# Block attention before two gated layers on one core: the head pairs of the attention taken two at a time, with the planner pricing each change of TensorE tiling

## The chip, the cores and the metric

One core of a Trainium2 chip runs the whole kernel. The metric is the device time of one execution in microseconds (us); the time before is the median of three runs, 610.3 us (610.02 to 610.71).

## What is computed

The reference, cut to what matters (B 2, H 8, S 768, D 64, block 32, window 16):

```
k_sum = k.reshape(B, H, nb, block, D).max(axis=3)
v_sum = v.reshape(B, H, nb, block, D).mean(axis=3)
scores_l = where(|i - j| < window, scale * q @ k.T, -1e9)
scores_s = scale * q @ k_sum.T + log(block)
a = softmax(concat(scores_l, scores_s))
x = a @ concat(v, v_sum)              # 1536 tokens x 512
h = x @ w_in;  g = h * clip(h + 3, 0, 6) / 6;  x = g @ w_out
h = x @ w_in2; g = h * cos(h);                 out = g @ w_out2
```

All is float32. The two layers have 512 inputs, 2048 inner units and 512 outputs.

## The kernel before, in words

**Attention.** Heads are taken in pairs: a pair's two heads lie on partitions 0 to 63 and 64 to 127, and there are four pairs (p) for each of two batches (b). The 768 tokens are cut into three parts (h) of 256, so there are 24 units (b, h, p). Only keys near the diagonal count, so each 64 query rows meet 120 columns: 96 keys (CW) of their window and 24 block maxima. A unit (`att`, L505) runs: `score` on TensorE (L511 to L518, eight small products of 64 rows by 64 columns, two instructions each, so 16 records) into the two PSUM tiles s; four times a masked minimum on VectorE (L529) and an exponential on ScalarE that also adds up its row (L537); a small addition on GpSimd (L546), the reciprocal (L551) and the scaling (L555, GpSimd or VectorE); four transposes (`trans`, L562) into t, a copy to pt (L567, ScalarE or VectorE); `pv` (L569 to L574, 16 records, 120 rows by 64 columns) into o; and the split of the result into a rounded high part xh (L580) and a remainder xl (L582).

**Loads and sums.** K, V and Q come by DMA from SP's queue (`load_k`, `load_v`, `load_q`, L453 to L468). At the first part of a batch, `k_prep` (L494) takes the block maxima of K on VectorE (L497) and `vsum_pe` (L470) the block means of V on TensorE: 24 small records (L477), a copy, a second product of two records (L482), another copy; `fill` (L489) then spreads the means into vw on GpSimd or ScalarE.

**Layers.** The 1536 tokens form three blocks of 512 (four tiles of 128). In each of two layers and for each of four groups of four chunks of 128 inner units, every block runs `g1` (L657: 12 products for each chunk, three for each quarter of the 512 inputs, so the first quarter needs head pair 0 only), `post` (L676, the gate on ScalarE, VectorE and GpSimd), and `g2` (L726, four output tiles of 12 products). The first block is cut in two halves of 256 tokens. The weights are loaded and converted chunk by chunk in two halves each (`weights`, L609; L618, L622, L627 and the splits). A block needs the attention of its own tokens only: block 0 needs parts 0 and 1 of batch 0, block 1 part 2 of batch 0 and part 0 of batch 1.

**Order.** `Plan` (L121) works out, before the kernel is built, when each operation starts on which engine, from the costs and priorities written at each `op` call and in the table T (L77): at each moment an engine takes the ready operation with the lowest priority whose buffers are free. Each engine, and SP's queue of DMAs, then runs its list in that order. The units stand in the order of the priorities: in batch 0 those of part 1 run interleaved with those of part 0, one pair behind; the rest follow part by part. Where the plan leaves TensorE idle before T's `busy` (42 us), `run` (L337) puts small products on the identity there (`idle`, L434), whose results nobody reads. Buffers are rings: z (Q) 3, e (the scores) 3, sm 4, pt 2, vs 2, r 2, and single PSUM tiles for t and o.

Of the kernel before, what the change touches and what calls it, by code (L numbers as in the profile page):

```python
# [14 lines left out]
ACTF = mybir.ActivationFunctionType  # L15
ALU = mybir.AluOpType
AX = mybir.AxisListType

P = 128
# [43 lines left out]
def consts():  # L63
# [53 lines left out]
class Op:  # L117
    __slots__ = ("engs", "fn", "prio", "port", "seq", "wait", "after", "ready", "takes", "uses", "start", "eng", "took")


class Plan:  # L121
# [10 lines left out]
    def op(self, engs, fn, prio, r=(), w=(), take=(), port=0.0):  # L132
        o = Op()
        o.engs, o.fn, o.prio, o.port, o.seq = engs, fn, prio, port, len(self.ops)
# [87 lines left out]

    def refine(self):
# [19 lines left out]
    def order(self):  # L243
# [6 lines left out]
        free["DMA"] = T["d0"]  # L250

# [11 lines left out]
        while events:  # L263
# [11 lines left out]
            for e in names:  # L275
# [79 lines left out]
def body(ctx: ExitStack, tc: tile.TileContext, q, k, v, w_in1, w_out1, w_in2, w_out2, ident_d, mask_d, avg_d, out):  # L355
# [34 lines left out]
    c_r = slots("r", 2, [P, TOK], later=T["n2"])  # L390
# [62 lines left out]
    def load_q(b, h, p, prio):  # L453
        z = Buf(c_z)
        dma(lambda: z.t, lambda: q[b, p][:, HT * P * h:HT * P * h + HT * P], 0.54, prio, w=[z], take=[z])
        return z
# [13 lines left out]
    def vsum_pe(vw, prio):  # L470

        bank, x, y = Buf(c_h), Buf(c_vs), Buf(c_y)

        def mm(e):
            for s in range(NS):
                a, g = 2 * (NS - 1 - s), s % 4 * QD
                nc.tensor.matmul(out=bank.t[g:g + QD, 0:P], lhsT=avg[0:CW, a:a + QD], rhs=vw.t[0:CW, s, :],  # L477
                                 start=(s < 4), stop=(s >= NS - 4), tile_position=(0, g))

        op({"PE": 0.85}, mm, prio, r=["avg", (vw, 0)], w=[bank], take=[bank, x, y])  # L480
        op({"ACT": 0.2, "DVE": 0.2}, lambda e: copy(e, y.t, bank.t[:, 0:P]), prio, r=[bank], w=[y])
        op({"PE": 0.25}, lambda e: nc.tensor.matmul(out=bank.t[CW:P, P:2 * P], lhsT=avg[:, AW:AW + QD], rhs=y.t,  # L482
                                                    start=True, stop=True, tile_position=(0, CW)),
           prio, r=["avg", y], w=[bank])
        op({"ACT": 0.2, "DVE": 0.2}, lambda e: copy(e, x.t[CW:CE, :], bank.t[CW:CE, P:2 * P]), prio, r=[bank],
           w=[(x, 0), (x, 1)])
        return x

    def fill(x, vw, prio):  # L489
        op({"POOL": 1.5, "ACT": 1.55},  # L490
           lambda e: copy(e, vw.t[CW:CE, :, :], x.t[CW:CE, :].rearrange("p (u f) -> p u f", u=1).to_broadcast([NB, NS, P])),
           prio, r=[(x, 0), (x, 1)], w=[(vw, CW)], take=[vw])
# [12 lines left out]
    def att(b, h, p, kw, z, vw, prio, banks):  # L505
        sp = [Buf(banks) for _ in range(2)]
        e_, sm, pt, tp, res = Buf(c_e), Buf(c_sm), Buf(c_pt), Buf(c_t), Buf(c_o)
        N4 = 2 * HT
        subs = [(i, u, o) for i in range(HT) for u in range(2) for o in range(2)]

        def score(e):  # L511
            for i, u, o in subs:
                f = slice(D * o, D * o + D)
                a = i * P + u * SUB
                nc.tensor.matmul(  # L515
                    out=sp[o].t[u * SUB:u * SUB + SUB, i * CE:i * CE + CE], lhsT=z.t[f, a:a + SUB],
                    rhs=kw.t[f, 2 * (HT * h + i) + u, :], start=True, stop=True,
                )  # L518

        op({"PE": 0.58}, score, prio,  # L520
           r=[z, (kw, "own"), (kw, "sum")], w=sp, take=[*sp, e_, sm])
        for i in range(HT):
            t = HT * h + i
            mk = mask[:, 0 if t == 0 else (2 if t == TB - 1 else 1), :]
            for o in range(2):
                x = 2 * i + o
                op(
                    {"DVE": 0.2},
                    lambda e, i=i, o=o, x=x, mk=mk: nc.vector.tensor_tensor_reduce(  # L529
                        out=e_.t[:, x, :], in0=sp[o].t[:, i * CE:i * CE + CE], in1=mk,  # L530
                        scale=-0.125, scalar=3.0e38, op0=ALU.add, op1=ALU.min, accum_out=sm.t[:, x:x + 1],
                    ),
                    prio, r=[sp[o], "masks"], w=[(e_, x), (sm, x)],
                )
                op(
                    {"ACT": 0.38},
                    lambda e, x=x: nc.scalar.activation(  # L537
# [286 lines left out]
```

## Time and profile before

| what | value |
|---|---|
| median of the runs | 610.3 us (610.02 to 610.71) |
| the profiled execution | 610.45 us |
| its span, first to last instruction | 608.7 us |
| TensorE (PE) busy | 602.1 us, 99% |
| VectorE (DVE) busy | 387.2 us, 64% |
| ScalarE (ACT) busy | 268.8 us, 44% |
| GpSimd (POOL) busy | 347.0 us, 57% |
| records of products on the identity | 146, the last at 45.10 us |
| granted TensorE clock | 1.00 throughout |

The busy times are sums over a span with two very different stages: attention mixed with the first blocks of the first layer (up to 118 us), and the layers alone. Matmul records overlap their successors, so what one costs TensorE is read from its start to the start of the next.

### The profile page before, as it was taken

Reading aid. Unit: us, or ns where it says so; the run is one execution under the profiler, and the core shown is the slowest. Engines: PE = TensorE matmul, PEld = TensorE weight load, DVE = VectorE, ACT = ScalarE, POOL = GpSimd, SP = SyncE. Lnnn points to the kernel's source line nnn. Section 1 sums busy time; section 2 is a strip of 40 time slices with the busy share of each in tenths; the row PEclk is TensorE's granted clock in tenths of the full one; section 3 lists DMA queues with packets and bytes.
Section 4 is the critical chain, followed back from the end, with each engine's and each line's share of the span. In section 5 each row is a group of like instructions: output and inputs, shape, how many; then the busy total and the mean of one; then the engine's idle time right before and its main releaser. Section 6 shows DMA issues by size and latency. Waiting matters only on the chain.

```text
span 608.7 us, 9662 instructions
## 1 busy us (share of the span) xinstructions
PE 602.1 (99%) x3636; PEld 498.6 (82%) x3636; DVE 387.2 (64%) x724; ACT 268.8 (44%) x585; POOL 347.0 (57%) x366
## 2 busy tenths in 40 slices
PE   9999999999999999999999999999999999999997
PEld 8878877788888888888888888888888888888886
DVE  3599894443852258523993589857984897574562
ACT  2698886533421114301351547654752363343240
POOL 2588784555853438623688398656864577443340
PEclk9999999999999999999999999999999999999999
DMA  9978950042420004300440013301320020000112
GB/s 224 269 240 246 255 184 22 1 138 70 138 70 0 1 7 167 105 0 1 140 137 0 1 69 104 104 2 68 105 103 2 1 103 1 1 2 0 70 42 97
DMA packets 28334, 50.07 MB, mean 82 GB/s; under 512 B 14464, under 2 KB 17920, under 8 KB 28288
## 3 DMA queue, kind: packets, MB, share of 16 engines
q1 hardware_dynamic: 28144, 49.40, 26.4%
q8 instruction: 28, 0.46, 0.3%
q14 instruction: 18, 0.15, 0.1%
q10 hardware_dynamic: 144, 0.07, 0.0%
HBM read 46.31 MB, written 3.15 MB: 81 GB/s over the span
## 4 chain that ended last, share of the span: by engine, by line
PE 94%; DVE 2%; POOL 1%; ACT 1%; issue 1%; DVEq 0%; POOLq 0%; ACTq 0%
PE acc L743 25%; PE s L743 18%; PE h L667 8%; PE h L668 8%; PE h L669 8%; PE o L669 3%; PE t L669 3%; PE o L667 3%; PE t L667 3%; PE o L668 3%; PE t L668 3%; PE acc L434 2%; PE s L515 2%; PE o L573 2%; PE t L564 2%; PE h L477 1%
## 5 line engine op out<-in xcount | busy, mean ns | idle before, releaser
L405 POOL TENSOR_SCALAR g<-r 128x512 fp32r<-128x512 f32 (+1 forms) x81 | 61.9, 764 | 135.4 <-DVE r L718 40.8
L410 POOL TENSOR_TENSOR g<-r,g 128x512 fp32r<-128x512 f32 (+1 forms) x73 | 100.5, 1377 | 7.3 <-ACT g L403 2.8
L699 ACT ACTIVATE n<-h,bias 128x512 f32<-128x512 f32 (+1 forms) x60 | 39.3, 656 | 141.3 <-PE h L669 139.3
L743 PE MATMUL acc<-g,w 128*128 128x512 f32 (+1 forms) x432 | 96.0, 370 | 0.0
L667 PE MATMUL h<-xh,w 128*128 128x512 f32 (+1 forms) x240 | 92.5, 386 | 0.0
L668 PE MATMUL h<-xl,w 128*128 128x512 f32 (+1 forms) x240 | 90.0, 375 | 0.0
L669 PE MATMUL h<-xh,w 128*128 128x512 f32 (+1 forms) x240 | 90.0, 375 | 0.0
L743 PEld LDWEIGHTS acc<-g,w 128*128 128x128 f32 x432 | 75.3, 188 | 14.3 <-issue 0.8
L703 DVE SCALAR_TENSOR_TENSOR r<-n,h 128x512 f32<-128x512 f32 (+1 forms) x60 | 38.7, 646 | 56.8 <-ACT n L699 31.0
L743 PE MATMUL acc<-w,g 128*128 128x512 f32 x288 | 69.2, 389 | 0.0
L743 PE MATMUL s<-w,g 128*128 128x512 f32 x288 | 69.2, 389 | 0.0
L410 POOL TENSOR_TENSOR w<-cf,w 128x512 fp32r<-128x512 f32 x44 | 64.1, 1460 | 3.3 <-ACT w L403 1.6
L743 PEld LDWEIGHTS acc<-w,g 128*128 128x128 f32 x288 | 54.1, 188 | 11.2
L743 PEld LDWEIGHTS s<-w,g 128*128 128x128 f32 x288 | 54.0, 188 | 11.2
L627 DVE SCALAR_TENSOR_TENSOR cf<-cu,cf 128x512 uint32<-128x512 uint32 x64 | 60.0, 955 | 0.4
L618 ACT ACTIVATE cu<-raw 128x512 f32<-128x512 f32 x64 | 42.9, 670 | 38.5 <-DVE cf L627 23.7
L622 DVE TENSOR_SCALAR cf<-raw 128x512 uint32<-128x512 uint32 x64 | 47.3, 755 | 11.8 <-POOL w L410 11.6
L667 PEld LDWEIGHTS h<-xh,w 128*128 128x128 f32 x240 | 45.1, 188 | 9.9 <-issue 1.7
L711 POOL TENSOR_SCALAR n<-n 128x512 f32<-128x512 f32 x45 | 31.8, 707 | 37.3 <-ACT n L699 37.2
L669 PEld LDWEIGHTS h<-xh,w 128*128 128x128 f32 x240 | 45.1, 188 | 8.2
L668 PEld LDWEIGHTS h<-xl,w 128*128 128x128 f32 x240 | 45.1, 188 | 7.8
L405 POOL TENSOR_SCALAR w<-cf 128x512 fp32r<-128x512 f32 x41 | 31.4, 770 | 30.3 <-DVE cf L627 23.2
(95 smaller groups left out, 1054.7 us busy)
## 6 DMA issues: line engine op xcount, KB each, us to landing
raw<-in_w_in_dram SPq DMA_DIRECT2D x32, 512.0 KB, 4.1
raw<-in_w_out_dram SPq DMA_DIRECT2D x32, 512.0 KB, 3.7
kw<-in_k_dram SPq DMA_DIRECT2D x8, 576.0 KB, 6.0
vw<-in_v_dram SPq DMA_DIRECT2D x8, 576.0 KB, 9.3
z<-in_q_dram SPq DMA_DIRECT2D x24, 128.0 KB, 5.7
out_dram<-part SPq DMA_DIRECT2D x8, 256.0 KB, 2.0
out_dram<-kw SPq DMA_DIRECT2D x3, 256.0 KB, 2.0
out_dram<-kw SPq DMA_DIRECT2D x2, 128.0 KB, 1.7
```

The costliest lines, as they stand in the source:

```text
L405: eng[e].tensor_scalar(out=out, in0=in_, scalar1=scale, scalar2=0.0, op0=ALU.mult, op1=ALU.add)
L410: eng[e].tensor_tensor(out=out, in0=in0, in1=in1.bitcast(F32), op=ALU.subtract)
L618: lambda e, raw=raw, u=u: nc.scalar.activation(out=u.t, in_=raw.t.bitcast(F32)[:, :, 1], func=ACTF.Prelu, scale=2.0 ** -112, alpha=2.0 ** 32),
L622: lambda e, raw=raw, f=f: eng[e].tensor_scalar(out=f.t.bitcast(U32), in0=raw.t[:, :, 0], scalar1=2.0 ** -29, scalar2=7.0, op0=ALU.mult, op ...
L627: lambda e, u=u, f=f: nc.vector.scalar_tensor_tensor(out=f.t.bitcast(U32), in0=u.t.bitcast(U32), scalar=3, in1=f.t.bitcast(U32), op0=ALU.l ...
L667: nc.tensor.matmul(out=o, lhsT=wh, rhs=hi, start=(kk == 0), stop=False)
L668: nc.tensor.matmul(out=o, lhsT=wh, rhs=lo, start=False, stop=False)
L669: nc.tensor.matmul(out=o, lhsT=wl, rhs=hi, start=False, stop=(kk == KT - 1))
L699: op({"ACT": t(fixed, 0.43)}, lambda e: nc.scalar.activation(out=out(), in_=in_(), func=func, **kw), pr, r=rd, w=wr, take=take)
L703: op({"DVE": t(0.09, 0.56)}, lambda e: nc.vector.scalar_tensor_tensor(out=out(), in0=a(), scalar=s, in1=b(), op0=o0, op1=o1), pr, r=rd, w= ...
L711: op({"POOL": t(0.16, 0.47), "DVE": t(0.07, 0.265)}, lambda e: eng[e].tensor_scalar(out=n(), in0=n(), scalar1=1.0, scalar2=-MAGIC, op0=ALU ...
L743: nc.tensor.matmul(out=o, lhsT=l, rhs=r, start=(c == 0 and z == 0), stop=(c == GS - 1 and z == 2))
```

## The change

Attention takes pairs of head pairs: `att` now gets one or two of them (ny). The 24 units become 13: part 0 of batch 0 as pair 0, pair 1, then pairs 2 and 3 together; from there on two pairs each. One `score` call issues 32 records for two pairs, and one `pv` call 32 records; transposes and their copies stay one call for each pair. Every exponential of the second pair is taken without its row sum, and one VectorE reduction over 4 x 120 elements takes the place of its four row sums. `vsum_pe` works on two V tiles: 48 records in its first call, and one second product of twice the columns. Q for two pairs comes by one DMA, and the copies to xh and xl are of twice the width. At part 0 of a batch, K and V are loaded two by two. The ring sizes and T change with it. The plan gets a price for each change of tiling on TensorE.

```diff
-    A0=6.982, AS=1.584, mask=-12.92, kp=-20.41, qp=-33.47, lk=-17.33, lq=-11.81, lv=-4.43, vs=33.64, vss=-16.92,
-    vsp=-29.27, wl=-1.64, wc=-25.07, g0=20.77, gi=7.33, pp=27.42, fill=-9.73, DVE=1.348, POOL=0.497, cold=5, d0=0.9,
-    warm=9, tail=1, lagq=1, nraw=3, ncf=2, n=5, w2=2, n2=3, g2=3, nz=3, busy=42, slack=0.2, vpe=-7.47, avg=-27.4,
+    A0=5.118, AS=1.568, mask=-8.22, kp=-14.19, qp=-15.92, lk=-15.36, lq=-11.42, lv=-4.09, vs=37.77, vss=27.87,
+    vsp=-18.03, wl=-15.78, wc=-15.19, g0=20.42, gi=5.51, pp=17.22, fill=-28.29, DVE=1.348, POOL=0.572, cold=5, d0=0.9,
+    warm=9, tail=1, lagq=3, nraw=3, ncf=2, n=5, w2=2, n2=3, g2=3, nz=2, nr=1, busy=42, slack=0.2, vpe=-45.26,
+    avg=-8.5,
...
+    def change(a, b):
+        if a == b:
+            return 0.0
+        return (0.165 if a > 1 else 0.0) + (0.19 if b > 1 else 0.1 if b else 0.0)
...
+                if e == "PE":
+                    cost += self.change(mode, o.mode)
+                    mode = o.mode
...
-    c_z = slots("z", T["nz"], [P, HT * P], pool=ap)
+    c_z = slots("z", T["nz"], [P, 2, HT * P], pool=ap)
-    c_vs = slots("vs", 2, [P, P], pool=ap)
-    c_y = slots("y", 1, [P, P], pool=ap)
+    c_vs = slots("vs", 1, [P, 2, P], pool=ap)
+    c_y = slots("y", 1, [P, 2, P], pool=ap)
-    c_e = slots("e", 3, [P, 2 * HT, CE], pool=ap)
-    c_sm = slots("sm", 4, [P, 4 * HT])
+    c_e = slots("e", 2, [P, 4 * HT, CE], pool=ap)
+    c_sm = slots("sm", 2, [P, 8 * HT])
-    c_r = slots("r", 2, [P, TOK], later=T["n2"])
+    c_r = slots("r", T["nr"], [P, TOK], later=T["n2"])
...
-        op({"PE": 0.85}, mm, prio, r=["avg", (vw, 0)], w=[bank], take=[bank, x, y])
+        op({"PE": 1.36}, mm, prio, r=["avg", *((vw, 0) for vw in vws)], w=[bank], take=[bank, x, y], mode=4)
...
-        op({"PE": 0.58}, score, prio,
-           r=[z, (kw, "own"), (kw, "sum")], w=sp, take=[*sp, e_, sm])
+        op({"PE": 0.41 * ny}, score, prio,
+           r=[z, *((kw, x) for kw in kws for x in ("own", "sum"))], w=sp, take=[*sp, e_, sm], mode=2)
...
+            add = x < N4
             op(
-                    {"ACT": 0.38},
+                {"ACT": 0.38 if add else 0.2},
...
+                    **(dict(accum_out=sm.t[:, N8 + x:N8 + x + 1]) if add else {}),
...
+            if y:
+                op({"DVE": 0.55},
+                   lambda e, y=y, a=a: nc.vector.tensor_reduce(
+                       out=sm.t[:, a], in_=e_.t[:, y * N4:y * N4 + N4, :], axis=AX.X, op=ALU.add),
+                   prio, r=[(e_, x) for x in xs], w=sums, port=0.3)
...
-        op({"PE": 0.62}, pv, prio, r=[pt, (vw, 0), (vw, CW)], w=[res], take=[res])
+        op({"PE": 0.44 * ny}, pv, prio, r=[*pts, *((vw, x) for vw in vws for x in (0, CW))], w=[res], take=[res], mode=3)
...
-    for p in range(NP + T["lagq"]):
-        units += [(0, 0, p)] * (p < NP) + [(0, 1, p - T["lagq"])] * (p >= T["lagq"])
-    units += [(b, h, p) for b in range(B) for h in range(NH) for p in range(NP) if b or h > 1]
+    units = [(0, 0, 0, 1), (0, 0, 1, 1), (0, 0, 2, 2)]
+    units += [(b, h, p, 2) for b in range(B) for h in range(NH) for p in range(0, NP, 2) if b or h]
...
+        both = (p, p + 1) if h == 0 and p % 2 == 0 else ()
+        for y in both:
+            kws[y], ks = load_k(b, y, pr + (y - p) * AS * HT * (ny < 2) + T["lk"])
+            k_prep(kws[y], ks, pr + T["kp"])
+        z = load_q(b, h, p, ny, pr + T["lq"])
+        for y in both:
+            vws[y] = load_v(b, y, pr + T["lv"])
+        if both:
+            x = vsum_pe([vws[y] for y in both], pr + T["vpe"])
+            for y in both:
+                fill(x, y - p, vws[y], pr + T["fill"])
```

## Rows read from the trace of the kernel before

**Rows 1.** Busy time by stretch: stretch, length, each engine's busy us (instructions), clock, DMA share, GB/s.

```profile
30.00:46.00 16.00, 14.64 (x219) 12.26 (x217) 15.65 (x47) 14.89 (x46) 13.31 (x15) 1.00 0.79 241
46.00:94.00 48.00, 47.40 (x668) 39.73 (x669) 44.21 (x163) 42.13 (x152) 36.62 (x44) 1.00 0.78 219
94.00:118.00 24.00, 24.00 (x246) 17.81 (x244) 9.50 (x47) 14.20 (x48) 12.38 (x16) 1.00 0.03 8
118.00:604.00 486.00, 486.00 (x2146) 402.42 (x2145) 304.25 (x402) 184.04 (x291) 273.92 (x269) 1.00 0.17 57
```

**Rows 2.** Waits of PE from 46 us to the end: us, times, longest.

```profile
PE s L515 <- DVE sm L529: 0.3, 1, 0.3
PE t L564 <- POOL e L555: 0.2, 1, 0.2
```

**Rows 3.** Timeline of PE, 0 to 42 us: start, first start to last end, instruction.

```profile
19.03 4.90 PE L434 MATMUL acc<-ident 128*128 128x64 f32 x42
23.86 0.86 PE L477 MATMUL h<-vw,avg 96*32 96x128 f32 x24
...
29.84 1.45 PE L434 MATMUL acc<-ident 128*128 128x64 f32 x12
...
35.14 0.39 PE L667 MATMUL h<-xh,w 128*128 128x256 f32 x1
```

**Rows 4.** Timeline of PE around one score group and one pv group, 59 to 61.5 us.

```profile
59.22 0.64 PE L515 MATMUL s<-kw,z 64*64 64x120 f32 x16
59.79 0.38 PE L667 MATMUL h<-xh,w 128*128 128x256 f32 x1
60.01 0.28 PE L668 MATMUL h<-xl,w 128*128 128x256 f32 x1
60.13 0.28 PE L669 MATMUL h<-xh,w 128*128 128x256 f32 x1
...
60.49 0.28 PE L669 MATMUL h<-xh,w 128*128 128x256 f32 x1
60.70 0.69 PE L573 MATMUL o<-pt,vw 120*64 120x64 f32 x16
61.31 0.39 PE L667 MATMUL h<-xh,w 128*128 128x256 f32 x1
```

**Rows 5.** Timeline of PE in windows that cut a group short, and one whole.

```profile
63.30 0.54 PE L515 MATMUL s<-kw,z 64*64 64x120 f32 x12
...
63.30 0.64 PE L515 MATMUL s<-kw,z 64*64 64x120 f32 x16
...
60.70 0.51 PE L573 MATMUL o<-pt,vw 120*64 120x64 f32 x10
...
79.54 0.64 PE L477 MATMUL h<-vw,avg 96*32 96x128 f32 x16
```

**Rows 6.** Groups of PE's instructions from 46 to 118 us: count, busy us, mean ns.

```profile
L573 PE MATMUL o<-pt,vw 120*64 120x64 f32 x272 | 11.7, 228 | 0.0
...
L515 PE MATMUL s<-kw,z 64*64 64x120 f32 x238 | 9.8, 275 | 0.5 <-DVE sm L529 0.3
...
L477 PE MATMUL h<-vw,avg 96*32 96x128 f32 x96 | 3.4, 277 | 0.0
L482 PE MATMUL h<-y,avg 128*32 128x128 f32 x8 | 1.6, 285 | 0.0
```

**Rows 7.** VectorE: a group of 30 to 94 us, one of 94 to 125, two reductions in the timeline.

```profile
L627 DVE SCALAR_TENSOR_TENSOR cf<-cu,cf 128x512 uint32<-128x512 uint32 x14 | 15.2, 1088 | 0.0
...
L529 DVE CUSTOM_DVE_ANT_0 e<-s,mask 128x120 f32<-128x120 f32 x16 | 3.6, 279 | 1.9 <-PE s L515 1.9
...
59.51 1.00 DVE L497 TENSOR_REDUCE ks<-kw 128x12 f32<-128x384 f32 x2
```

**Rows 8.** ScalarE: the reads of the row sums, a group of 30 to 94 us.

```profile
L537 ACT ACTIVATION_READ_ACCUMULATOR e<-e,sm 128x1 f32 x59 | 11.1, 188 | 0.0
```

**Rows 9.** SP's queue, timeline: start, us from first to last issue's end.

```profile
27.29 0.44 SPq L437 DMA_DIRECT2D vw<-in_v_dram  x1
```

More of the change, by code (lines that the diff above doesn't have):

```diff
@@ L117 @@
 class Op:
-    __slots__ = ("engs", "fn", "prio", "port", "seq", "wait", "after", "ready", "takes", "uses", "start", "eng", "took")
+    __slots__ = ("engs", "fn", "prio", "port", "seq", "wait", "after", "ready", "takes", "uses", "start", "eng", "took", "mode")
 class Plan:
@@ L562, in trans @@
-        def trans(e):
-            for x in range(N4):
-                nc.tensor.transpose(out=tp.t[0:CE, x * P:(x + 1) * P], in_=e_.t[:, x, :], identity=ident)
-        op({"PE": 0.44}, trans, prio, r=[(e_, x) for x in range(N4)], w=[tp], take=[tp, pt])
-        op({"ACT": 0.49, "DVE": 0.6}, lambda e: copy(e, pt.t[0:CE, :], tp.t[0:CE, :]), prio, r=[tp], w=[pt])
-        def pv(e):
-            for i, u, o in subs:
-                f = slice(D * o, D * o + D)
-                a, c = (2 * i + o) * P + u * SUB, i * P + u * SUB
-                nc.tensor.matmul(out=res.t[f, c:c + SUB], lhsT=vw.t[0:CE, 2 * (HT * h + i) + u, f],
-                                 rhs=pt.t[0:CE, a:a + SUB], start=True, stop=True)
@@ L576, in att @@
-        op({"PE": 0.62}, pv, prio, r=[pt, (vw, 0), (vw, CW)], w=[res], take=[res])
+            for y in range(ny):
+                for i, u, o in subs:
+                    f = slice(D * o, D * o + D)
+                    a, c = i * P + u * SUB, (y * HT + i) * CE
+                    nc.tensor.matmul(
+                        out=sp[o].t[u * SUB:u * SUB + SUB, c:c + CE], lhsT=z.t[f, y, a:a + SUB],
+                        rhs=kws[y].t[f, 2 * (HT * h + i) + u, :], start=True, stop=True,
+                    )
@@ new lines, in att, with trans @@
+        for y in range(ny):
+            xs = range(y * N4, y * N4 + N4)
+            sums = [(sm, N8 + x) for x in xs]
+            a = slice(N8 + y * N4, N8 + y * N4 + N4)
+            if y:
[3 more added lines that the diff above has]
+                   prio, r=[(e_, x) for x in xs], w=sums, port=0.3)
+            op(
+                {"POOL": 0.2},
+                lambda e, a=a: nc.gpsimd.tensor_scalar(
+                    out=sm.t[:, a], in0=sm.t[:, a], scalar1=1.0, scalar2=1e-9, op0=ALU.mult, op1=ALU.add
+                ),
+                prio, w=sums,
+            )
+            op({"DVE": 0.09}, lambda e, a=a: nc.vector.reciprocal(out=sm.t[:, a], in_=sm.t[:, a]), prio, w=sums)
+            op(
+                {"POOL": 1.05, "DVE": 0.57},
+                lambda e, y=y, a=a: eng[e].tensor_tensor(
+                    out=e_.t[:, y * N4:y * N4 + N4, :], in0=e_.t[:, y * N4:y * N4 + N4, :],
+                    in1=sm.t[:, a].rearrange("p (x u) -> p x u", u=1).to_broadcast([P, N4, CE]), op=ALU.mult,
+                ),
+                prio, r=sums, w=[(e_, x) for x in xs], port=0.5,
+            )
+            def trans(e, y=y, xs=xs):
+                for x in xs:
+                    c = (x - y * N4) * P
+                    nc.tensor.transpose(out=tps[y].t[0:CE, c:c + P], in_=e_.t[:, x, :], identity=ident)
+            op({"PE": 0.425}, trans, prio, r=[(e_, x) for x in xs], w=[tps[y]], take=[tps[y], pts[y]], mode=1)
+            op({"ACT": 0.49, "DVE": 0.6}, lambda e, y=y: copy(e, pts[y].t[0:CE, :], tps[y].t[0:CE, :]), prio, r=[tps[y]],
+               w=[pts[y]])
@@ new lines, in pv @@
+        def pv(e):
+            for y in range(ny):
+                for i, u, o in subs:
+                    f = slice(D * o, D * o + D)
+                    a, c = (2 * i + o) * P + u * SUB, (y * HT + i) * P + u * SUB
+                    nc.tensor.matmul(out=res.t[f, c:c + SUB], lhsT=vws[y].t[0:CE, 2 * (HT * h + i) + u, f],
+                                     rhs=pts[y].t[0:CE, a:a + SUB], start=True, stop=True)
+        op({"PE": 0.44 * ny}, pv, prio, r=[*pts, *((vw, x) for vw in vws for x in (0, CW))], w=[res], take=[res], mode=3)
@@ L577, in att @@
         j, i = divmod(b * TB + HT * h, QT)
         c = slice(i * P, (i + HT) * P)
[L579 to L583 removed]
+        hi, lo = xh[j][:, p:p + ny, c], xl[j][:, p:p + ny, c]
@@ L585, in body, with both @@
+        his, los = ([(x, j, p + y, t) for y in range(ny) for t in range(i, i + HT)] for x in ("xh", "xl"))
+        def both():
+            return res.t[:, 0:ny * HT * P].rearrange("p (y c) -> p y c", y=ny)
+        op({"ACT": 0.07 + 0.21 * ny, "DVE": 0.07 + 0.27 * ny}, lambda e: copy(e, hi, both()), prio, r=[res], w=his)
+        op({"DVE": 0.06 + 0.27 * ny}, lambda e: sub(e, lo, both(), hi), prio, r=[res, *his], w=los)
     A0, AS = T["A0"], T["AS"]
```

131 lines of the change are left out of this document (52 added, 79 removed).

## The prediction

> **What bounds the kernel.** I read first the busy time by stretch [rows 1]: from 118 to 604 us TensorE is busy without a gap, and from 94 to 118 as well; from 46 to 94 it lacks 0.6 us in 48. The granted clock is 1.00, the 2.4 GHz level, in every stretch, so no time is to be had from the clock. Next the waits of TensorE from 46 us on [rows 2]: two, 0.5 us together. So from 46 us to the end TensorE works through a fixed list in a fixed order, and whatever is taken out of that list ends the kernel earlier by as much, as long as the other engines still deliver in time. Before 46 us it is otherwise. The timeline [rows 3] shows products on the identity, which nobody reads: 42 of them between 19.03 and the V sums at 23.86, 12 more from 29.84 and 14 later ones. There TensorE is waiting for loads and for other engines, and taking products out gives only more of these. The layers begin at 35.14.
>
> The second thing to see in [rows 1] is VectorE: 15.65 of 16 us up to 46, 44.21 of 48 up to 94, then only 9.50 of 24. It is nearly full exactly where the change gives it more to do.
>
> **What a group of small products costs TensorE.** In the stretch of [rows 4], products of the layers on 256 columns start 0.12 us apart (60.01 to 60.13). A score group takes 0.57 us from its start to the next instruction (59.22 to 59.79). The product before a small group takes 0.21 until the group starts (60.49 to 60.70), 0.09 too much, and the first after it 0.22 (59.79 to 60.01), 0.10 too much. A pv group takes 0.61 (60.70 to 61.31). Inside a group the pace is quicker than these figures: cutting the score group after 12 of 16 records shortens it by 0.10, so 0.025 a record and 0.40 for 16; cutting a pv group after 10 shortens it by 0.18, so 0.03 a record and 0.48 for 16 [rows 5]. What is left is the price of entering and leaving: 0.57 + 0.19 - 0.40 = 0.36 us for scores, 0.61 + 0.19 - 0.48 = 0.32 for pv. For the V sums, 24 records take 0.86 and 16 take 0.64 [rows 3, 5], so 0.0275 a record and 0.66 for 24. Their ends overlap the successor by 0.07, as the score group's do (0.64 against 0.57), so the group takes 0.79, and its price is 0.79 + 0.19 - 0.66 = 0.32.
>
> **The change on TensorE.** After 46 us stand 238 score records (14 whole groups and the rest of one), 272 of pv (17 groups), 96 of V sums (4 groups) and 8 of their second product (4 groups) [rows 6]. Two pairs in one call leave the records and take away every second group: 7 x 0.36 = 2.5, 8.5 x 0.32 = 2.7, 2 x 0.32 = 0.6. Of the second products two go, at least the 0.19 at their edges, 0.4; their columns remain. Sum 6.2 us. Some groups already stand directly behind another small group and have no edge to the layers, so I take 5.5; the ends are 6.2 and, if the next paragraphs go wrong, nothing. The transposes stay as they are, one call a pair, and cost what they did. The groups before 46 us save as much each, but there it turns into waiting.
>
> **The ramp.** The new priorities put part 0 of batch 0 first: before, part 1 came in between, and the last V of the batch was issued only at 27.29 [rows 9], behind the first weights (its priority 18.4 against 13.7 for the first chunk; after the change 7.3 against 7.1 for the first chunk and 8.5 for the second, worked out from the two tables T). So pairs 2 and 3 should have their V some us earlier and the first half of block 0 can start earlier. What this can give at most is the slack after 29.84: 26 products on the identity at 0.12 (1.45 for 12 [rows 3]) is 3.1 us, and the idle time of 30 to 46 is 1.36 [rows 1], together 4.5; the 4.83 us from 19.03 to 23.86 could come on top, since both V tiles are now fetched before the first sum. Against it stands that a pair of pairs waits for the later of two loads, that its z is freed only after both scores, with the loads behind it in SP's queue, and that only two e tiles of double size are left. I take -3.0, two thirds of the 4.5; the ends are -9.3 and a loss of two further waits of 4.83, that is +9.7.
>
> **VectorE.** It gets 11 reductions over 480 elements. The nearest row is a reduction over 384, 1.00 us for two [rows 7]; so between 0.50 and 0.63 each, and I take 0.56, 6.2 us in all. Behind 94 us only 16 of the 96 masked minima are left, four units [rows 7], so 20 of the 24 units come before; in the new form these hold nine reductions, 9 x 0.56 = 5.0 us, against 0.35 + 3.79 = 4.1 us idle between 30 and 94 [rows 1]. And that stretch is to become some us shorter. What can give way: the weights of the second group, converted early. The 14 conversions of 30 to 94 us [rows 7] are six more than the first group's four chunks need, 1.09 us each, 6.5 us that can move past 94, where VectorE is half idle. I count +1.5 us of TensorE waiting for VectorE, between 0 and 4.
>
> **ScalarE** loses 44 reads of row sums, at most 0.19 us each [rows 8]; it has 42.13 of 48 us in the middle stretch [rows 1] and doesn't set the pace, so I count nothing; if VectorE were short, the copies that may go to either would move over. The wider copies to xh and xl and the 11 Q loads fewer move the same bytes: nothing, hidden behind TensorE's list. One r tile in place of two before 118 us: r is held for one chunk's gate, and block 0's chunks pass between attention groups, further apart than a gate lasts, so nothing; without that cover g1 would wait for its PSUM bank.
>
> **Sum** for the profiled execution: 610.45 - 5.5 - 3.0 + 1.5 = 603.45. That execution lies 0.15 above the median of the runs, so 603.3 us.
>
> **Rivals.**
> *VectorE becomes the bound up to 94 us.* For it: the fill of [rows 1] and the reductions. Against it: the conversions that can move. Then TensorE gains only behind 94, where four score groups become two and at least as many pv groups, 2 x 0.36 + 2 x 0.32 = 1.4, the ramp gains nothing, and the stretch grows by 5.0 - 4.1 = 0.9: 610.45 + 0.9 - 1.4 = 609.95. The Trainium skill, page "VectorE: DVE Perf Modes", section "Rules for kernel authors", speaks for this one: it calls the tensor_reduce the slowest operation of that engine and advises against it on a hot path. By that rule the sum would be this 609.95 and not 603.3; the trace agrees that it is slow, half a microsecond for 384 elements [rows 7], but the path is hot only as far as the conversions can't move.
>
> *The ramp gets longer, and the kernel slower.* Pairs taken together wait for the later of their two V loads and fills. Place: the first pv of pairs 2 and 3 of part 0, then the first of part 1, which needs the pt tiles of that one. Price: a wait like that of 19.03 to 23.86 twice, 9.7 us. Then 610.45 + 9.7 - 5.5 = 614.6. It decides from the point at which the ramp loses more than the 5.5; one such wait would still leave about no change. Against it: the priorities of K and V.
>
> *The ramp gives all of its slack* and VectorE doesn't hold anything up: 610.45 - 5.5 - 4.5 and half of the 4.83 is 598.0.
>
> *The change doesn't save the edges*, because what costs is each group's first and last records wherever they stand. Then only the ramp and VectorE remain, 610.45 - 3.0 + 1.5 = 609.0. The even pace inside a group [rows 5], across changes of row and column halves, speaks against it.
>
> **Chances.** The forecast, 600 to 607: 0.62. The full ramp: 0.13. VectorE as the bound: 0.12, half of it just past the border of a measurable gain. The long ramp: 0.10. No edges saved: 0.03. A measurement of this kernel can tell 0.2%, 1.2 us, from no change. Faster by more than that: 0.62 + 0.13 + 0.06 + 0.02 = 0.83; within: 0.07; slower: 0.10. The range leaves out the long ramp, half of the VectorE case and the far end of the full ramp: 596.5 to 609.1.
>
> **What would show it.** In the trace after: 13 score groups, 11 of them of 32 records and 1.04 us long, pv groups of 32 in 1.17 us, with the same 0.09 and 0.10 at their edges; 11 new reductions of 0.50 to 0.63 us on VectorE and 52 reads of row sums on ScalarE; the first product of a layer before 35 us and fewer than 146 products on the identity; the waits of TensorE after 46 us below 2 us. The forecast is wrong if TensorE waits for VectorE by more than 4 us between 30 and 94, if the layers begin later than 35 us, or if a group of 32 takes twice a group of 16.

## The result, and the profile after

The changed kernel takes 618.58 us (median of four runs), the kernel before 610.5 in the same comparison: 1.0126 times as long, with a 95% interval of 1.0111 to 1.0142. It is slower by about 8 us where the forecast was 7 faster. One of the four runs, 637.6 us, is of a slower kind that the kernel before shows too (628 us in other comparisons); the medians in this document count such runs (without it this one is 617.67), the ratios leave them out. The profiled execution took 619.48 us with a span of 617.7 and a mean clock of 0.994; the remaining two took 617.65 and 617.67 at a mean clock of 1.00, so the loss is there without a lower clock.

Busy time by stretch of the kernel after (stretch, length, busy us and instructions of PE, PEld, DVE, ACT, POOL, then the granted clock, the DMA share and GB/s), beside [rows 1]:

```profile
0.00:30.00 30.00, 28.83 (x340) 27.01 (x340) 11.84 (x54) 11.37 (x35) 7.54 (x19) 1.00 0.91 236
30.00:46.00 16.00, 15.62 (x265) 13.79 (x264) 14.85 (x51) 14.71 (x42) 12.53 (x14) 1.00 0.74 236
46.00:94.00 48.00, 42.83 (x584) 37.38 (x581) 41.62 (x127) 34.41 (x91) 32.58 (x42) 0.93 0.76 218
70.00:80.00 10.00, 8.79 (x127) 7.05 (x128) 7.79 (x40) 6.94 (x24) 3.84 (x6) 0.66 0.71 204
94.00:118.00 24.00, 24.00 (x269) 20.03 (x268) 11.78 (x64) 14.88 (x49) 12.07 (x18) 1.00 0.09 24
118.00:131.00 13.00, 13.00 (x120) 10.62 (x119) 5.81 (x25) 7.50 (x21) 5.97 (x9) 1.00 0.00 1
131.00:612.00 481.00, 481.00 (x2150) 398.27 (x2150) 306.60 (x404) 182.88 (x289) 277.05 (x267) 1.00 0.17 57
```

From 46 to 94 us TensorE now lacks 5.2 us of 48 (0.6 before), and its mean clock there is 0.93 of full speed. The window cut closer, from 70 to 80 us, has a clock of 0.66. From 94 us on TensorE is full again, as before. The waits of TensorE from 46 us on, against [rows 2], no longer make half a microsecond but 4.8:

```profile
PE t L595 <- POOL e L585: 1.6, 1, 1.6
PE s L538 <- issue: 1.5, 1, 1.5
PE t L595 <- DVE e L585: 1.0, 1, 1.0
PE s L538 <- DVE sm L551: 0.5, 1, 0.5
PE h L708 <- DVE r L744: 0.2, 1, 0.2
```

The ramp, from the timeline of PE (start, first start to last end, instruction), against [rows 3]:

```profile
8.87 8.47 PE L447 MATMUL acc<-ident 128*128 128x64 f32 x74
17.18 0.60 PE L595 MATMUL t<-ident,e 128*120 128x128 f32 x4
17.71 0.64 PE L538 MATMUL s<-kw,z 64*64 64x120 f32 x16
...
21.19 3.56 PE L447 MATMUL acc<-ident 128*128 128x64 f32 x30
24.68 1.52 PE L492 MATMUL h<-vw,avg 96*32 96x128 f32 x48
...
30.40 0.69 PE L606 MATMUL o<-pt,vw 120*64 120x64 f32 x16
...
37.20 1.05 PE L538 MATMUL s<-kw,z 64*64 64x120 f32 x32
38.19 2.45 PE L447 MATMUL acc<-ident 128*128 128x64 f32 x20
40.56 1.15 PE L606 MATMUL o<-pt,vw 120*64 120x64 f32 x32
```

The first thing to see is 74 records on the identity in a row, 8.47 us. The transposes at 17.18 that stand behind them have had their input since 12.67, by the timeline of DVE:

```profile
11.77 0.90 DVE L585 TENSOR_TENSOR e<-e,sm 128x480 f32<-128x480 f32 x1
```

So TensorE makes products that nobody reads for 4.5 us while work is ready. The groups of the kernel after show the same in sum, 236 such records against 146, and the new reductions:

```profile
L447 PE MATMUL acc<-ident 128*128 128x64 f32 x236 | 27.9, 275 | 0.0
...
L560 ACT ACTIVATION_READ_ACCUMULATOR e<-e,sm 128x1 f32 x52 | 9.8, 188 | 0.0
...
L572 DVE TENSOR_REDUCE sm<-e 128x4 f32<-128x480 f32 x11 | 7.1, 644 | 3.1 <-ACT e L560 3.1
```

**An account of TensorE.** I went through the timeline of PE from start to start up to the last pv group and put each stretch to one of three: attention's products (with the 18 at the very start), products of the layers, and slack, which is waits and products on the identity. Slack is split at the first product of a layer. "Rest" is the span less attention's products and slack.

The last pv group itself counts to the rest. All runs but the first two are described in the next section.

| profiled execution | span | attention's products | slack before the first layer product | slack after it | rest |
|---|---|---|---|---|---|
| before | 608.7 | 52.7 | 16.8 | 2.1 | 537.1 |
| after | 617.7 | 48.9 | 21.3 | 11.2 | 536.3 |
| before, divisor 0.23 (e2) | 607.1 | 54.0 | 14.4 | 1.3 | 537.4 |
| after, divisor 0.23 (e1) | 610.6 | 48.7 | 15.0 | 9.7 | 537.2 |
| e1 with the old table (e6) | 609.0 | 48.6 | 15.4 | 7.9 | 537.1 |
| e1 with four single units first (e9) | 606.6 | 48.6 | 12.0 | 9.5 | 536.5 |
| single units under the new planner (e18) | 619.7 | 57.1 | 15.3 | 10.1 | 537.2 |

The rest is the same within 1.1 us, so the account closes. The larger groups save 3.8 us; the slack grows by 13.6, by 4.5 ahead of the first layer product and by 9.1 behind it.

### The profile page after: what moved, and what is told of

It reads as the page before. It is cut to its first block, busy times and chain, and to the rows that moved or that the text cites. A ratio compares the mean times of both kernels' runs of the same rounds, so it can differ in the third digit from the quotient of the medians.

```text
span 617.7 us, 9723 instructions
## 1 busy us (share of the span) xinstructions
PE 606.8 (98%) x3718; PEld 508.0 (82%) x3718; DVE 393.3 (64%) x723; ACT 265.8 (43%) x523; POOL 347.7 (56%) x366
## 4 chain that ended last, share of the span: by engine, by line
PE 90%; DVE 6%; POOL 1%; ACT 1%; issue 1%; DVEq 0%; POOLq 0%
PE acc L784 24%; PE s L784 18%; PE h L708 8%; PE h L710 8%; PE h L709 8%; PE t L710 3%; PE o L709 3%; PE o L710 3%; PE t L709 3%; PE t L708 3%; PE o L708 3%; PE acc L447 3%; DVE cf L668 2%; PE o L606 1%; PE s L538 1%
## 5 line engine op out<-in xcount | busy, mean ns | idle before, releaser
L418 POOL TENSOR_SCALAR g<-r 128x512 fp32r<-128x512 f32 (+1 forms) x84 | 64.1, 763 | 127.2 <-DVE r L744 39.3
L423 POOL TENSOR_TENSOR g<-r,g 128x512 fp32r<-128x512 f32 (+1 forms) x83 | 111.3, 1341 | 8.5 <-ACT g L416 3.0
L423 POOL TENSOR_TENSOR w<-cf,w 128x512 fp32r<-128x512 f32 x43 | 62.7, 1463 | 3.5 <-ACT w L416 1.6
L668 DVE SCALAR_TENSOR_TENSOR cf<-cu,cf 128x512 uint32<-128x512 uint32 x64 | 61.7, 978 | 3.3 <-ACT cu L659 2.7
L784 PEld LDWEIGHTS acc<-w,g 128*128 128x128 f32 x288 | 54.1, 188 | 11.2
L784 PEld LDWEIGHTS s<-w,g 128*128 128x128 f32 x288 | 54.1, 188 | 11.2
L418 POOL TENSOR_SCALAR w<-cf 128x512 fp32r<-128x512 f32 x44 | 33.4, 764 | 33.4 <-DVE cf L668 24.2
L663 DVE TENSOR_SCALAR cf<-raw 128x512 uint32<-128x512 uint32 x64 | 43.9, 701 | 9.2 <-POOL w L423 9.1
L752 POOL TENSOR_SCALAR n<-n 128x512 f32<-128x512 f32 x36 | 25.9, 718 | 39.1 <-ACT n L740 39.1
```

The costliest lines, as they stand in the source:

```text
L418: eng[e].tensor_scalar(out=out, in0=in_, scalar1=scale, scalar2=0.0, op0=ALU.mult, op1=ALU.add)
L423: eng[e].tensor_tensor(out=out, in0=in0, in1=in1.bitcast(F32), op=ALU.subtract)
L663: lambda e, raw=raw, f=f: eng[e].tensor_scalar(out=f.t.bitcast(U32), in0=raw.t[:, :, 0], scalar1=2.0 ** -29, scalar2=7.0, op0=ALU.mult, op ...
L668: lambda e, u=u, f=f: nc.vector.scalar_tensor_tensor(out=f.t.bitcast(U32), in0=u.t.bitcast(U32), scalar=3, in1=f.t.bitcast(U32), op0=ALU.l ...
L752: op({"POOL": t(0.16, 0.47), "DVE": t(0.07, 0.265)}, lambda e: eng[e].tensor_scalar(out=n(), in0=n(), scalar1=1.0, scalar2=-MAGIC, op0=ALU ...
L784: nc.tensor.matmul(out=o, lhsT=l, rhs=r, start=(c == 0 and z == 0), stop=(c == GS - 1 and z == 2))
```

## The experiments

"e1" to "e18" are the runs in their order. The comparison is always with the kernel before on the same chip (610.3 to 610.5 us).

**Products on the identity.** `run` puts int((gap - 0.2) / 0.11) calls into a planned gap, but a call is two records of 0.115 us each (8.47 us for 74 records), so it fills about twice the gap. In e1 (changed kernel) and e2 (kernel before):

```diff
-                    for _ in range(int((o.start - last - T["slack"]) / 0.11)):
+                    for _ in range(int((o.start - last - T["slack"]) / 0.23)):
```

> The changed kernel with its order untouched; only the number of products on the identity put into a planned gap of TensorE is worked out with 0.23 us each (two records of 0.115 us, as the trace shows: 74 records from 8.87 to 17.18) in place of 0.11. Theory A, the fillers: they take twice the planned gap, 208 records past the first five us where about 100 were meant, some 12 us too many, and push the whole ramp back; then the time falls by 6 to 12 us, to 606 to 612. Theory B, the data: the pairs wait for their loads and V sums in any case; the fillers turn into waits and the time stays at 616 to 618. Theory C, VectorE with its 11 reductions sets the pace from 50 to 78 us: 615 to 618, since that stretch doesn't begin earlier.

> The kernel before with the same edit. It has 108 such records past the first five us, about 52 too many, 6 us. Theory A: it gains too, 2 to 6 us, to 604 to 608, so that part of the loss of the change is the same flaw met oftener. Theory B and C: 610.

e1 took 613.97 us, ratio 1.0055 (1.0035 to 1.0076): some 4.5 us of the 8 are back. e2 took 609.02, ratio 0.9986 (0.9967 to 1.0006): at most a small gain, 1.5 us by the medians. So of the 8 us between the two kernels the overrun accounts for about 3, and 5 stay when both have the right divisor. Timeline of PE in e1:

```profile
8.88 4.01 PE L447 MATMUL acc<-ident 128*128 128x64 f32 x34
12.72 0.61 PE L595 MATMUL t<-ident,e 128*120 128x128 f32 x4
13.26 0.64 PE L538 MATMUL s<-kw,z 64*64 64x120 f32 x16
...
19.37 0.86 PE L492 MATMUL h<-vw,avg 96*32 96x128 f32 x24 [0.34 <-DMA vw<-in_v_dram]
...
23.65 0.69 PE L606 MATMUL o<-pt,vw 120*64 120x64 f32 x16 [0.27 <-POOL vw L418]
```

The transposes start at 12.72, the first pv at 23.65 and no longer at 30.40. That part of the loss is shown. The other 5 us against e2 are not explained by it: e1's slack behind the first layer product is still 9.7 us against 1.3.

In e3 these products are left out altogether (`if False:` in place of the test ahead of that loop).

> The changed kernel, order untouched, with no products on the identity after the first nine. Theory A: as the run with the right number or a little better, 604 to 612, as long as the clock holds; if the granted clock falls in the ramp the small products there take up to twice as long and half of the gain is lost. Theory B: 616 to 618 at the full clock.

616.35 us, ratio 1.0104 (1.0083 to 1.0126): worse than e1. Windows of e3:

```profile
0.00:10.00 10.00, 4.80 (x34) 4.27 (x34) 2.55 (x10) 1.28 (x1) 1.50 (x9) 0.88 0.93 218
10.00:20.00 10.00, 5.83 (x88) 4.74 (x92) 6.33 (x38) 5.19 (x24) 2.25 (x5) 0.50 1.09 281
20.00:30.00 10.00, 7.10 (x94) 4.80 (x86) 6.76 (x26) 8.56 (x24) 7.06 (x9) 0.67 1.02 301
30.00:40.00 10.00, 9.01 (x136) 7.22 (x135) 6.47 (x25) 7.65 (x17) 7.08 (x8) 0.76 0.66 223
40.00:50.00 10.00, 6.76 (x99) 5.36 (x101) 8.52 (x30) 8.52 (x28) 7.00 (x10) 0.93 0.89 250
```

TensorE stands idle for about half of the first 20 us; the granted clock falls to 0.50 (the 1.2 GHz level) from 10 to 20 us and is at 0.93 only from 40 us on. So the useless products earn something: without any of them the kernel takes 2 to 3 us more than e1, with twice too many of them some 4.5 more.

**VectorE's reductions.** In e4 ScalarE adds up the second pair's rows as it did before, in the order of the changed kernel, and a copy of four numbers stands for the reduction. e7 is the same with the divisor 0.23, planned anew with these costs. e12 keeps e1's order and lets the reductions read 4 columns of 120, with nothing in their place (the sum of the other columns is left out, and a constant is added so that the values stay bounded). The edit shown is that of e4:

```diff
-                    **(dict(accum_out=sm.t[:, N8 + x:N8 + x + 1]) if add else {}),
+                    accum_out=sm.t[:, N8 + x:N8 + x + 1],
...
-                   lambda e, y=y, a=a: nc.vector.tensor_reduce(
-                       out=sm.t[:, a], in_=e_.t[:, y * N4:y * N4 + N4, :], axis=AX.X, op=ALU.add),
+                   lambda e, a=a:
+                   nc.vector.tensor_copy(sm.t[:, a], sm.t[:, a]),
```

> The changed kernel, order untouched: ScalarE adds up the second pair's exponentials as it did before (44 reads of row sums back, 8 us on ScalarE), and a copy of four columns stands in for each of VectorE's 11 reductions (some 5 us less on VectorE). Theory C: the 5 us that TensorE idles between 60 and 78 us shrink by 3 to 5, to 612 to 615. Theories A and B: within 2 us of the changed kernel, 616 to 619.

> As e1, and ScalarE adds up the second pair's exponentials as before, this time with the plan knowing it (0.38 us for each exponential, no reduction on VectorE), so that the whole order is worked out anew. Theory C: VectorE's reductions are a part of the rest; 608 to 611. Theories D and E: as e1 within 2 us, 612 to 616.

> Changed kernel with the divisor 0.23 and its order, but the 11 reductions of the second pair's exponentials read 4 columns of 120 in place of all (and 120 is added to these sums so that later values stay bounded): 0.65 us of VectorE each become about 0.1, and ScalarE gets nothing in their place. So the second pair's sums are left out, and 6 us of work are gone from VectorE, which the second run showed full from 50 to 70 us. The second run gave 613.97 us. Theory F (from 20 to 80 us the engines beside TensorE do as much as they can, so what TensorE saves turns into waits): 609 to 611 us, and the slack of TensorE (identity products and waits up to the last pv) falls by 3 to 5 us from 24.7. Theory E (the length of a unit's chain through the scaled exponentials on GpSimd): 612.5 to 614.5.

e4: 619.18 us, against 618.58. e7: 614.1, ratio 1.0053 (1.0032 to 1.0074). e12: 613.46, ratio 1.0065 (1.0038 to 1.0092), both against e1's 613.97. Seven microseconds of VectorE's work, moved or gone, change nothing that these intervals (some 1.5 us to either side) can tell, though VectorE is full in places of e1:

```profile
50.00:60.00 10.00, 7.83 (x94) 7.26 (x98) 10.00 (x32) 6.52 (x21) 7.19 (x11) 0.94 1.08 318
60.00:70.00 10.00, 8.38 (x158) 7.26 (x151) 10.00 (x38) 6.86 (x23) 6.13 (x10) 0.89 0.73 202
```

So the reductions aren't what costs: theory C falls, and theory F (all the engines beside TensorE are full) as far as it rests on VectorE. The Trainium skill, page "VectorE: DVE Perf Modes", section "Rules for kernel authors", would have one consider restructuring them on a hot path. Each takes 0.64 us here, and these three runs show no gain from taking them away in this kernel.

**Weights later, table of before, a third z tile.** All three with the divisor 0.23: e5 sets wc = -10, e6 takes the table T of the kernel before (with nz = 2, nr = 1), e8 sets nz = 3 and shortens a padding tile to make room.

```diff
-    warm=9, tail=1, lagq=3, nraw=3, ncf=2, n=5, w2=2, n2=3, g2=3, nz=2, nr=1, busy=42, slack=0.2, vpe=-45.26,
+    warm=9, tail=1, lagq=3, nraw=3, ncf=2, n=5, w2=2, n2=3, g2=3, nz=3, nr=1, busy=42, slack=0.2, vpe=-45.26,
...
-    cp.tile([P, 112], F32, name="after_x")
+    cp.tile([P, 32], F32, name="after_x")
```

> The changed kernel with the right number of products on the identity (as e1, 613.97) and one entry of T changed: wc from -15.19 to -10, so that the conversions of the weights stand 5 us later among VectorE's, ScalarE's and GpSimd's work. Theory D: the rest of the loss, TensorE's idle time from 40 to 72 us (9.7 us of waits in e1), comes from the order that the priorities of T make, in which conversions stand ahead of what attention waits for; then 606 to 611. Theory C, too much work on VectorE, and theory E, the pairs' own rings: no change against e1, 612 to 616.

> The changed kernel with the right number of products on the identity and the table T of the kernel before (ring sizes z 2 and r 1 kept). Theory D: T is at fault, not the pairs; 605 to 611. Theory E, what the pairs wait for (both loads, z and e tiles): no better than e1, 612 to 617.

> As e1, with three z tiles (Q for two pairs each) in place of two; a row of padding behind the x tiles is shortened to make room. Theory E: a score of a pair of pairs waits for Q, which is only fetched once the score two before has freed its tile (1.5 us before the score at 66 us in e1, 4.0 in e3); 609 to 612. Otherwise as e1, 613 to 615.

e5: 612.0 us, ratio 1.0032 (1.0021 to 1.0043); its interval overlaps e1's, and the 606 to 611 of theory D is missed. e6: 612.17, ratio 1.0021 (1.0009 to 1.0033), again short of D's 605 to 611. e8: 619.29, ratio 1.0144 (1.0127 to 1.0161). e6's account says why it gains 1.8 only: the slack goes from 24.7 to 23.3. e8 says nothing of z, for its layers took longer; that stands in the last section.

**Single units first, single rings.** e10 gives each pair its own tiles z, e and sm (four of half the size); e9 has them too and takes the first four units one pair at a time; e11 the first eight; e15 is e9 with the divisor 0.18. The edits of e9 at the rings and the units:

```diff
-    c_z = slots("z", T["nz"], [P, 2, HT * P], pool=ap)
+    c_z = slots("z", 4, [P, HT * P], pool=ap)
-    c_e = slots("e", 2, [P, 4 * HT, CE], pool=ap)
-    c_sm = slots("sm", 2, [P, 8 * HT])
+    c_e = slots("e", 4, [P, 2 * HT, CE], pool=ap)
+    c_sm = slots("sm", 4, [P, 4 * HT])
...
-    units = [(0, 0, 0, 1), (0, 0, 1, 1), (0, 0, 2, 2)]
+    units = [(0, 0, p, 1) for p in range(NP)]
```

> Changed kernel with the divisor 0.23, in which the first four units of block 0, part 0, are four single pairs of heads (their V sums, copies and second products one pair at a time too), each with tiles z, e and sm of its own; all the later units are pairs of pairs as changed. The second run (0.23 alone) gave 613.97 us. Theory E (a unit of two pairs has its eight minima, eight exponentials, two scalings and two transposes between its scores and its pv, and in the ramp nothing else is there to do meanwhile): the wait list loses what it held in the first 40 us, the first pv comes at about 18 to 20 us in place of 23.65, and the time is 606 to 609 us, below the 609.0 of the kernel before with the same divisor, for it keeps nearly all of the 5 us that the larger groups save. Rival (the growth sits in the steady stretch from 40 to 118 us, where VectorE is full, and not in the ramp): 611 to 613 us. Rival (the data sets the ramp): the same 612 to 614 us, with z or vw among the ends of the waits.

> Changed kernel with the divisor 0.23, units as changed, but every pair of heads of a unit has tiles z, e and sm of its own (four of each of half the size in place of two), so that a tile comes free as soon as its own pair is done; q comes by two DMAs for a unit in place of one. The second run (0.23 alone) gave 613.97 us. If a unit's late release of its shared tiles were what makes the waits: 609 to 611 us. Theory E (the length of a unit's own chain, which this leaves as it is): 612 to 615 us, with s<-issue and t<-POOL e still at the top of the wait list. It is also the control of the run before it, which has the same rings.

> As the run with four single units first, but parts 0 and 1 of block 0 are both made of single pairs: eight single units, then pairs of pairs. Four groups of scores and four of pv more than there are split in two, at 0.36 and 0.32 us of edges each: 2.7 us for four units. Theory E as it stands (only the first units of the ramp have nothing beside them): 1 to 3 us more than the run with four singles. If latency hurts well past the ramp: no more than the run with four, or less. If neither run gains against 613.97: the loss is not that of a long unit.

> The run with four single units first, its divisor 0.18 in place of 0.23: about 28% more products on the identity than a planned gap holds, so that the granted clock falls less after the first waits. That run gave 611.11 us, 608.4 to 608.8 us where the mean granted clock of the run was 0.994 or more and 611 to 613.6 us where it was below. If the clock is what is left of the loss: 608 to 610 us, with the clock at 1.0 in more of the runs. If the products that overrun push the ramp back by as much: 611 to 613 us.

e9: 611.11 us, ratio 1.0011 (0.9995 to 1.0028), 2 to 3 below e1 and above the 606 to 609 expected. e10: 612.55, ratio 1.0038 (1.0019 to 1.0057); up to half of e9's gain may come with the rings, but e10's interval overlaps both e1's and e9's. e11: 615.39, ratio 1.0106 (1.0048 to 1.0164): with more single units the time is longer again. e15: 611.9, ratio 1.0023 (1.0006 to 1.0039), no better than e9. The account of e9 says what it wins: 3 us of slack ahead of the first layer product, none behind it.

**The scaling, in both kernels.** e13 is e1, e14 is e2, with the scaling cut to 8 of 120 columns: most of the normalisation is left out (and the minima get a bound so that the values stay bounded). One line of e13's edit:

```diff
-                    out=e_.t[:, y * N4:y * N4 + N4, :], in0=e_.t[:, y * N4:y * N4 + N4, :],
+                    out=e_.t[:, y * N4:y * N4 + N4, 0:8], in0=e_.t[:, y * N4:y * N4 + N4, 0:8],
```

> Changed kernel with the divisor 0.23 and its order, but the scaling of the exponentials multiplies 8 columns of 120 in place of all (and the exponentials are made smaller by a bound on the minima, so that later values stay bounded): 1.08 us on GpSimd or about as much on VectorE, for each of 24 scalings, become about 0.3. So the normalisation of most columns is left out. It takes 0.8 us out of the chain of every pair, just ahead of the transposes that wait longest (t<-POOL e 3.0 us). The second run gave 613.97 us. Theory E: 608 to 610.5 us, the wait t<-POOL e gone. Theory F: some gain too, as 18 us of work go from GpSimd and VectorE: 609 to 612; the run of the kernel before with the same cut says how much of it is the change's own. If neither holds (the order or TensorE sets the time): 612.5 to 614.5.

> The kernel before with the divisor 0.23 and the same cut of the scaling to 8 columns (normalisation of most columns left out). Without the cut it gave 609.02 us. Theories E and F both say that the kernel before is bounded by TensorE from 34 us on (slack 1.3 us from there), so the cut helps only in the ramp: 607 to 609 us. If it gains as much as the changed kernel does by the same cut, then neither theory explains why the change lost.

e13: 612.14 us, ratio 1.0024 (1.0011 to 1.0037). e14: 606.4, ratio 0.9954 (0.9923 to 0.9985). The cut gives the changed kernel 1.4 to 1.8 us and the kernel before 2.6; in both cases the intervals with and without it overlap. There is no sign that a pair's chain is worth more in the changed kernel than in the kernel before, so theory E doesn't explain the loss.

**Order against units.** e16 is the kernel before with the changed kernel's T, e17 is e9 with the old T, e18 is the changed kernel with every unit a single pair and the old T; all with the divisor 0.23.

```diff
-    units = [(0, 0, 0, 1), (0, 0, 1, 1), (0, 0, 2, 2)]
-    units += [(b, h, p, 2) for b in range(B) for h in range(NH) for p in range(0, NP, 2) if b or h]
+    units = [(b, h, p, 1) for b in range(B) for h in range(NH) for p in range(NP)]
```

> The kernel before with the divisor 0.23 and the table T of the changed kernel (nz stays 3): single pairs of heads in the order that the new due times give. With its own table it gave 609.02 us; the changed kernel gave 613.97 with the new table and 612.17 with the old one. Theory G (the new table's order is worse on the chip for whatever units): 611 to 614 us. Theory E (the pairing of units itself costs the slack): 608 to 610 us.

> The run with four single units first, with the table T of the kernel before (nz = 2, nr = 1 as changed). With the new table it gave 611.11 us. Theory G: 608 to 610 us, as the old table took 1.8 us off the changed kernel. Theory E: 610.5 to 612 us.

> The changed kernel with the divisor 0.23, every unit a single pair of heads (score and pv groups of 16, V sums of 24), tiles z, e and sm for one pair each (four of each), and the table T of the kernel before: the units of the kernel before under the changed kernel's planner (which prices changes of tiling). The second pair's reduction never runs: ScalarE makes all sums. Theory E (the loss is that of paired units): 608 to 610.5 us, as the kernel before with the divisor 0.23 (609.02). Theory G or the priced changes of tiling (the order is worse whatever the units): 611.5 to 615 us.

| units, planner | old table | new table |
|---|---|---|
| single, planner of before | 609.02 (e2) | 614.4 (e16), ratio 1.0067 (1.0048 to 1.0087) |
| single, changed planner and rings | 620.87 (e18), ratio 1.0175 (1.0132 to 1.0217) | not tried |
| in pairs, changed planner and rings | 612.17 (e6) | 613.97 (e1) |
| four single, then pairs, changed planner, rings of e9 | 611.96 (e17), ratio 1.0027 (1.0017 to 1.0038) | 611.11 (e9) |

The new table costs the old units 5.4 us. Under the changed planner with the old table, pairs of pairs beat single pairs by 8.7 (e18's rings and its V sums, one at a time, differ from e6's too, so not all of it is the units); with the new table under the two planners, pairs and single pairs are level (613.97 and 614.4). No two runs that differ mainly in the units show that taking pairs together costs time, which points at the order. But the table isn't as clean as it looks. The entry `lagq` of T sets how far part 1 of batch 0 stands behind part 0 in the list of units of the kernel before; the new table has 3 there, which puts all of part 1 behind part 0, and the changed kernel doesn't read it and never mixes the two parts. So only the kernel before, e2 and e14 mix them. That lost mixing is a rival to the table and to the planner, and no run separates it. The windows of e18:

```profile
20.00:30.00 10.00, 7.03 (x133) 5.37 (x133) 4.31 (x23) 6.75 (x26) 6.93 (x9) 1.00 1.01 305
30.00:40.00 10.00, 9.66 (x95) 7.74 (x94) 9.61 (x24) 7.07 (x23) 7.21 (x7) 0.53 0.70 223
40.00:50.00 10.00, 7.61 (x98) 5.85 (x96) 8.21 (x21) 8.30 (x22) 7.86 (x9) 0.96 0.74 236
```

Idle time from 20 to 30 us is followed by ten at a clock of 0.53, near the 1.2 GHz level, and from 40 us on TensorE lacks time again. In the account, slack behind the first layer product is 1.3 and 2.1 us for the old units in their own order, parts mixed, and 7.9 to 11.2 in every other one, paired or single.

What stays open: which part of the change (the parts no longer mixed, the price of a change of tiling, the lower costs of score and pv, one tile each for vs and r) makes e18's order so much worse than e2's. These were not tried one by one, so the cause of the 5 us between e1 and e2 is narrowed down and not shown. Of the runs that compute everything, none is clearly faster than both kernels; the nearest is e2.

## Why the prediction was wrong

**Products on TensorE: right.** Forecast were 0.36 us for every second score group, 0.32 for pv and for V sums, 0.19 at least for a second product. In the timeline of PE after:

```profile
84.01 1.52 PE L492 MATMUL h<-vw,avg 96*32 96x128 f32 x48
85.46 0.98 PE L784 MATMUL acc<-g,w 128*128 128x256 f32 x6
86.37 0.62 PE L500 MATMUL h<-y,avg 128*32 128x256 f32 x2
86.92 0.62 PE L784 MATMUL acc<-g,w 128*128 128x256 f32 x3
...
92.03 1.15 PE L606 MATMUL o<-pt,vw 120*64 120x64 f32 x32
93.11 0.39 PE L708 MATMUL h<-xh,w 128*128 128x256 f32 x1
```

pv of two pairs takes 1.08 to the next start; twice 0.61 and one pair of edges (0.19) were 1.41, so 0.33 is saved. A score group (37.20 to 38.19) takes 0.99 for 2 x 0.57 + 0.19 = 1.33: 0.34. The V sums take 1.45 for 1.77: 0.32. In sum the whole kernel has 3.8 us less of attention's products (5.3 in e1 against e2, whose products are partly at a lower clock), where 5.5 was forecast for the time behind 46 us alone. The Trainium skill, page "TensorEngine Tiling (Array Packing)", section "Key Properties", says that a change of tiling mode drains the engine; the edges here fit that, 0.32 to 0.34 us saved for a pair of them.

**The ramp: wrong.** "I take -3.0", from priorities that fetch V earlier. SP's timeline after has the last V of the batch in this issue, against 27.29 before:

```profile
19.85 0.90 SPq L450 DMA_DIRECT2D vw<-in_v_dram  x2
```

So V did come early, but the first V sums did not use it: they start at 24.68 behind gaps that were filled twice over, and at 18.17 in e1. The first layer product came at 35.58 (35.14 before) with 21.3 us of slack ahead of it in place of 16.8: +4.5 where -3.0 stood in the sum. The premise that products on the identity mark waiting was wrong. For part of their time ready work stands behind them, which the pace of [rows 3] (1.45 us for 12 records) beside the divisor 0.11 would have shown.

**"Whatever is taken out of that list ends the kernel earlier by as much": wrong for a new list, and as large a miss.** It holds for an order in which layer work is always ready. The change replaces T, the planner and the order of the units, and so the list itself; behind the first layer product the slack rose by 9.1 us, from 2.1 to 11.2, where the sum had +1.5 for VectorE and nothing for the new order. The prediction counted it as a gain that part 1 no longer stands between the units of part 0; whether this is what took the ready work away was not tried. e16 measures what the new table, the lost mixing with it, does to the old units: 5.4 us. What of the order makes the slack stays open.

**VectorE: its size nearly right, its part nil.** A reduction takes 0.64 us against the 0.56 taken, 7.1 us in all; in e4, e7 and e12 no gain comes from taking it away.

**The clock: missed.** "No time is to be had from the clock" is true of the kernel before, but time can be lost by it. It is not the main part: the two runs of the changed kernel at a mean clock of 1.00 are 1.8 us shorter than the one at 0.994, and still 7 us longer than before. Timeline of PE in e1, the first pv of pairs 2 and 3, then a score group ahead of and one behind two waits:

```profile
35.18 1.15 PE L606 MATMUL o<-pt,vw 120*64 120x64 f32 x32
...
39.65 1.05 PE L538 MATMUL s<-kw,z 64*64 64x120 f32 x32
...
57.90 0.65 PE L595 MATMUL t<-ident,e 128*120 128x128 f32 x4 [1.66 <-POOL e L585]
59.06 2.08 PE L538 MATMUL s<-kw,z 64*64 64x120 f32 x32 [0.50 <-DVE sm L551]
```

The same 32 records take 1.05 us, and 2.08 after two waits. In e9 the runs with a mean clock of 0.994 or more took 608.4 to 611.0 us, those with 0.983 to 0.992 took 611.1 to 613.6.

**The rivals.** "The ramp gets longer, and the kernel slower" (614.6 us, chance 0.10) was the right side. Its mechanism was not what happened: the slack ahead of the first layer product grew by 4.5 us and not by 9.7, twice as much stands behind it, and in e1, without the overrun, the first pv of pairs 2 and 3 starts at 35.18 (above) with no wait for V or its fill. Of the signs named for a wrong forecast, the late layers and the waits above 2 us behind 46 came true; the lengths of the groups and the 52 reads came out as said, and the 11 reductions with 0.64 us just above the 0.50 to 0.63.

## What to carry to other kernels

Where an order is planned ahead, price an edit together with the order that it brings: put the new table under the old units and the old table under the new ones before you credit either, and see to it that no entry of the table also changes the list of units. Filler work must be sized by the measured length of what it issues, for what overruns delays ready work (e1) and what is missing let the clock fall (e3). Shorter groups on an engine are worth their saving only as far as other work is ready behind them; count the slack of the whole stretch, products on the identity included, and not the waits alone.

## What was not expected of the hardware

In one run the pace of products changed whose code was not touched. In e8 (one z tile more, a padding tile 80 floats shorter) the stretch from 200 to 300 us holds 439 products against 442 in e1, both at a clock of 1.00. That stretch and groups of it, first of e1, then of e8:

```profile
200.00:300.00 100.00, 100.00 (x442) 82.78 (x442) 51.06 (x65) 22.22 (x34) 48.38 (x48) 1.00 0.16 53
L708 PE MATMUL h<-xh,w 128*128 128x512 f32 x40 | 15.6, 389 | 0.0
```

```profile
200.00:300.00 100.00, 100.00 (x439) 82.17 (x439) 49.29 (x63) 21.69 (x34) 47.05 (x47) 1.00 0.17 53
L708 PE MATMUL h<-xh,w 128*128 128x512 f32 x38 | 15.0, 395 | 0.0
L710 PE MATMUL h<-xh,w 128*128 128x512 f32 x38 | 14.9, 392 | 0.0
L709 PE MATMUL h<-xl,w 128*128 128x512 f32 x38 | 14.8, 389 | 0.0
```

Its attention's products (49.3) and slack (25.4) leave 542.0 of its span of 616.7 us for the rest, some 5 more than the runs of the account. The tiles' places in memory are the suspect, but the third z tile also enters the plan; neither is shown, and which tile's place it would be was not tried.

Leaving TensorE idle can cost more than the idle time: e3, with no products on the identity, also runs 10 us at a clock of 0.50 and twenty at 0.67 to 0.76, where e1 has 1.00, 0.91 and 0.92.
